# Pooled attention with a feed-forward layer: one weight conversion step on ACT instead of DVE, roundings of weights at another place of a step, other due times in the first and last pairs

## The chip, the cores and the metric

The kernel runs on one core of a Trainium2 chip. The metric is the time of the program on the device in microseconds (us). The engines are PE (matrix multiply), DVE (vector), ACT (scalar and activation functions), POOL (GpSimd) and SP, which here only issues transfers.

## The reference

```python
# attention: B, H, S, D = 4, 8, 1152, 64; q and k are scaled by about 0.71
q_pool = q.reshape(B, H, S // 2, 2, D).mean(axis=3)
scores = scale * np.matmul(q_pool, k.transpose(0, 1, 3, 2))
scores = scores - np.max(scores, axis=-1, keepdims=True)
attn = np.exp(scores)
attn = attn / (np.sum(attn, axis=-1, keepdims=True) + 1e-09)
attn_out = np.matmul(attn, v)
# feed-forward: x is attn_out as 2304 tokens x 512; w_in 512 x 2048, w_out 2048 x 512
h = np.maximum(x @ w_in, 0.0)
return h * h @ w_out
```

All data are 32 bits. The kernel computes each product in three matmuls of rounded halves: a value x is split into a rounded high half and the low half x - high.

## The kernel before

The work has two parts. The **attention** part goes over 16 pairs of heads, n = 0 to 15, and in each over two halves of the pooled queries, e = 0 and 1; (n,e) is called a half pair here. For a pair, `prep` (four steps u) transposes keys and queries on PE into PSUM banks; `prep_high` on ACT and `prep_low` on DVE write the two halves. For a half pair, `scores` gives nine chunks c on PE, each in a PSUM bank; `evict` brings a chunk to SBUF, six of the nine on DVE (L381, with a running maximum) and three on ACT (L378); `max_copied` (L385) takes the maximum of those three. `max_fin` (L327), a transposition on PE (`max_turn`) and `max_rows` (L343) make of it the shift of the exponentials. ACT takes the exponentials in place, in six instructions (`expo`, L389). POOL adds exponentials of several chunks (`add`, L432), so that the sum (`total`, L439) needs fewer matmuls; the half pairs (n,0) have four additions, (n,1) three, pair 15 none and two. `pv` (L404) multiplies with the values; `total_x` (ACT, then DVE L452 and L453) inverts the sum, and `pv_x` (L465) writes the result into `xt`. PSUM has four banks for `scores`, `prep`, the maxima and the open sums together.

The **feed-forward** part goes over steps (i, f): block i of the tokens (256, then four of 512) and slice f of 128 of the 2048 inner columns, in five passes of 2, 3, 4, 4 and 3 slices over all blocks. A step is `layer1` (12 matmuls, then on ACT g = relu, square, and the rounded half `gh`, and `gl` on DVE) and `layer2` of the step two before it (12 matmuls for a full block). At the end of a pass over a block the accumulators are copied out of PSUM, by ACT in the first pass (L693), by DVE in the others (L695); the next block needs their banks. `split_x` makes the halves of a block of x, ACT (L160) and DVE (L161).

The weights come as whole 32-bit units u = 0 to 31 (512 columns of 128 rows; even u are of `w_in`, odd of `w_out`) and are converted by `convert`, six steps: L122 the absolute value, L124 a maximum, L127 a shift, L130 and L134 bits, L136 a product into `r`, which POOL then adds to (L138). Its buffer `a` is single: L122 of a unit writes what L136 of the unit before reads. `split_w` rounds the converted weight on ACT (L148) and subtracts, on DVE for u < 4 and on POOL after that (L149). Units 0 to 3 are converted in the attention part: 0 and 1 during pairs 0 to 2, 2 and 3 during pair 15. The others are converted one pass ahead of their use.

The order of the attention part is written by a planner: `at` gives every operation a due time from the tables `AT` (L21) and `BT` (L28), never earlier than the operations that it must follow, and `plan` (L503) emits them sorted by due time. Each engine works its queue in that order. In the feed-forward part (L716 to L743) the operations are traced step by step; a scheduler may reorder them on an engine, while a conversion step is kept behind all that is traced before it on its engine (`keep_in_program_order`).

Of the kernel before, what the change touches and what calls it, by code (L numbers as in the profile page):

```python
# [8 lines left out]
F32 = mybir.dt.float32  # L9
# [4 lines left out]
ACTF = mybir.ActivationFunctionType  # L14
ALU = mybir.AluOpType
# [10 lines left out]
    u3=2.1607, vs=0.025, x0=0.0686, x1=0.3357, xg=0.2377,  # L26
)
BT = dict(  # L28
    u0=2.461, u1=-0.052, u2=1.778, u3=2.34, c0=2.06, c1=2.959, c2=-0.148, c3=1.446, cs=0.404, x=-1.613,
    w0=-2.307, w1=-1.838, s0=-0.109, s1=-0.104, v0=0.619, v1=2.469, t0=-5.963, t1=-1.1, lastn=3, lv=-3.166,  # L30
    pq=-0.498, s2=0.089, s3=0.001, v2=-0.001, lastm=9, t2=-0.385, p0=1.161, p1=0.934, wd=0.681, w=0.073,
    v3=-0.582, t3=-1.202, p2=0.017, p3=-0.048, y0=0.536, y1=0.082, y2=0.119, y3=0.466, d0=0, d1=-0.024,
)
WARM = 24
SOON = 3
# [5 lines left out]
def kernel(  # L41
# [9 lines left out]
    nc = tc.nc  # L51
# [26 lines left out]
    def run(ctx, exact):  # L78
# [18 lines left out]
        WB = 6  # L97
        NU = 2 * KF
        NCV = 6
# [4 lines left out]
        def load_raw(u):  # L104
            f, half = divmod(u, 2)
            t = cv.tile([P, CW, 2], I32, tag="raw", name="raw", bufs=2)
            if half == 0:
                nc.sync.dma_start(out=t.rearrange("p (k f) e -> p k f e", k=KD),
                                  in_=WI[:, 2 * f * P:2 * (f + 1) * P].rearrange("(k p) (f e) -> p k f e", p=P, e=2))
            else:  # L110
                nc.sync.dma_start(out=t, in_=WO[f * P:(f + 1) * P, :].rearrange("p (d e) -> p d e", e=2))
            raw[u] = t

        def convert(u, part):
            if part == 0:
                cvt[u] = [cv.tile([P, CW], I32, tag="a", name="a"), cv.tile([P, CW], I32, tag="h", name="h", bufs=2),
                          wfp.tile([P, CW], F32, tag="r", name="r")]
            a, h, r = cvt[u]
            lo, hi = raw[u][:, :, 0], raw[u][:, :, 1]
            if part == 0:  # L120

                i = nc.vector.tensor_scalar(out=a, in0=hi, scalar1=0x7FFFFFFF, scalar2=None, op0=ALU.bitwise_and)  # L122
            elif part == 1:
                i = nc.vector.tensor_scalar(out=a.bitcast(F32), in0=a.bitcast(F32), scalar1=TINY, scalar2=None, op0=ALU.max)  # L124
            elif part == 2:

                i = nc.vector.tensor_scalar(out=a, in0=a, scalar1=3, scalar2=0x3FFFFFF8, op0=ALU.logical_shift_left,  # L127
                                            op1=ALU.bitwise_and)
            elif part == 3:
                i = nc.vector.scalar_tensor_tensor(out=h, in0=hi, scalar=-0x40000000, in1=a, op0=ALU.bitwise_and,  # L130
                                                   op1=ALU.bitwise_or)
            elif part == 4:

                i = nc.vector.tensor_scalar(out=a, in0=h, scalar1=-0x800000, scalar2=None, op0=ALU.bitwise_and)  # L134
            else:
                i = nc.vector.scalar_tensor_tensor(out=r, in0=lo.bitcast(U32), scalar=2.0 ** -52, in1=a.bitcast(F32),  # L136
                                                   op0=ALU.mult, op1=ALU.mult)
                nc.gpsimd.tensor_tensor(out=r, in0=r, in1=h.bitcast(F32), op=ALU.add)  # L138
                wf[u] = r
                del cvt[u], raw[u]  # L140
            return i

        def split_w(u, pool, tag, bufs):

            f, half = divmod(u, 2)
            x = wf.pop(u)
            w = pool.tile([P, 2, CW], F32R, tag=tag, name=tag, bufs=bufs)
            nc.scalar.copy(out=w[:, 0], in_=x)  # L148
            (nc.vector if u < CU else nc.gpsimd).tensor_tensor(out=w[:, 1], in0=x, in1=w[:, 0], op=ALU.subtract)  # L149
            (wo if half else wi)[f] = w  # L150
# [18 lines left out]
        with ExitStack() as a:  # L169
# [5 lines left out]
            lv = a.enter_context(tc.tile_pool(name="lv", bufs=2))  # L175
# [461 lines left out]
        wp = ctx.enter_context(tc.tile_pool(name="wp", bufs=WB))  # L637
# [75 lines left out]
        work = {}  # L713
# [10 lines left out]
        for n in range(len(steps) + 2):  # L724
            for u, j in work.get(n, []):
                if j < NCV:
                    if j == 0 and u + 1 < NU:
                        load_raw(u + 1)
                    tc.keep_in_program_order(convert(u, j))
                else:  # L730
                    split_w(u, wp, "w" + "io"[u % 2], WB)
            if n < len(steps):
                i, f, p = steps[n]
                if f == P0[p] + 1 and n + PASS[p] - 1 < len(steps):
                    split_x(turns[turns.index((i, p)) + 1][0], xh_p)
                layer1(i, f)
            if n >= 2:
                layer2(*steps[n - 2][:2])
            if n == NB * PASS[0] and not exact:
                judge()  # L740

# [2 lines left out]
    with ExitStack() as c:  # L744
        run(c, False)
# [33 lines left out]
```

## Time and profile before

| | us |
|---|---|
| runs | 786.03, 786.09, 787.78 (median 786.09) |
| profiled execution | 785.6 |
| its span | 783.5 |
| PE busy | 740.1 (94%) |
| DVE busy | 589.4 (75%) |
| ACT busy | 498.2 (64%) |
| POOL busy | 400.4 (51%) |

The span runs from the first to the last instruction of the profiled execution; 2.1 us lie around it. The attention part lasts to about 375 us, the feed-forward part from there to the end. A timeline row gives the start, the duration, the operation, and in brackets how long the engine had been idle before it and what ended that.

### The profile page before, as it was taken

To read this page: it belongs to the slowest core of one execution; us is meant where nothing else is said; L and a number is where in the kernel's file an instruction comes from. 1 tells how busy PE (TensorE), PEld (TensorE's weight loads), DVE (VectorE), ACT (ScalarE), POOL (GpSimd) and SP (SyncE) were. 2 spreads that over 40 slices of the span, in tenths; PEclk is the share of its full clock that TensorE was granted. 3 is DMA by queue.
4 is the path that set the end of the run, shared out by engine and by line. 5 is a ranking of instruction groups with operands and counts; after the bars stand their busy time and mean duration, and the time that the engine had idled before them with its cause. 6 is when DMAs were issued, how large, how long until landed. Compare 5 with 4: busy or idle time off the path is not lost.

```text
span 783.5 us, 14050 instructions
## 1 busy us (share of the span) xinstructions
PE 740.1 (94%) x5514; PEld 579.8 (74%) x5514; DVE 589.4 (75%) x1095; ACT 498.2 (64%) x794; POOL 400.4 (51%) x176
## 2 busy tenths in 40 slices
PE   8768999999999999989989999999999999999996
PEld 7546666777776667666767788888888888888885
DVE  6988999999999999987997997676645655434432
ACT  3748888888888888974856654454444544444431
POOL 1758999999999999985253343122121311110000
PEclk9999999999999999999999999999999999999998
DMA  9233333333222333000121121011100100000312
GB/s 264 63 88 89 92 92 92 92 91 85 78 68 63 77 91 92 32 32 28 55 80 55 55 80 54 28 55 54 54 28 27 55 28 27 1 2 5 103 55 85
DMA packets 62091, 50.80 MB, mean 65 GB/s; under 512 B 39232, under 2 KB 49472, under 8 KB 62016
## 3 DMA queue, kind: packets, MB, share of 16 engines
q1 hardware_dynamic: 60656, 47.59, 22.1%
q10 hardware_dynamic: 1360, 2.23, 0.9%
q8 instruction: 45, 0.74, 0.4%
q14 instruction: 30, 0.25, 0.1%
HBM read 45.09 MB, written 4.72 MB: 64 GB/s over the span
## 4 chain that ended last, share of the span: by engine, by line
PE 68%; DVE 20%; ACT 4%; issue 4%; POOL 3%; DVEq 0%; POOLq 0%; ACTq 0%
PE o L687 22%; PE h L652 21%; PE s L404 11%; PE s L362 10%; DVE p L381 6%; DVE pm L385 4%; POOL ts L432 3%; ACT p L389 2%; PE s L439 1%; DVE xlo L161 1%; PE s L251 1%; DVE r L136 1%; DVE a L134 1%; DVE h L130 1%; PE s L624 1%
## 5 line engine op out<-in xcount | busy, mean ns | idle before, releaser
L389 ACT ACTIVATE p<-p,nb 128x864 f32<-128x864 f32 x192 | 184.4, 1009 | 31.1 <-DVE nb L343 31.0
L652 PE MATMUL h<-xhi,wi 128*128 128x512 f32 (+1 forms) x600 | 170.0, 368 | 0.0
L687 PE MATMUL o<-wo,gh 128*128 128x512 f32 x540 | 166.7, 390 | 1.2 <-DVE part L695 1.2
L138 POOL TENSOR_TENSOR r<-r,h 128x512 f32<-128x512 f32 x32 | 46.1, 1439 | 205.0 <-DVE r L136 193.3
L381 DVE TENSOR_SCALAR_CACHE_REDUCE p<-s 128x576 f32<-128x576 f32 x192 | 138.4, 755 | 11.5 <-PE s L362 7.0
L404 PE MATMUL s<-p,vt 128*64 128x288 f32 x1080 | 143.6, 409 | 0.0
L362 PE MATMUL s<-qq,kk 64*128 64x288 f32 x1728 | 132.1, 301 | 7.4 <-ACT p L378 3.1
L362 PEld LDWEIGHTS s<-qq,kk 64*128 64x128 f32 x1728 | 118.5, 186 | 23.4 <-issue 13.4
L432 POOL TENSOR_TENSOR ts<-p 128x1728 f32<-128x1728 f32 x31 | 120.3, 3880 | 25.4 <-ACT p L389 24.2
L652 PEld LDWEIGHTS h<-xhi,wi 128*128 128x128 f32 x600 | 109.6, 188 | 19.9
L432 POOL TENSOR_TENSOR ts<-ts,p 128x1728 f32<-128x1728 f32 x31 | 122.2, 3943 | 3.7 <-ACT p L389 1.3
L659 DVE TENSOR_TENSOR gl<-g,gh 128x512 fp32r<-128x512 f32 (+1 forms) x80 | 55.3, 692 | 89.3 <-ACT gh L658 89.0
L687 PEld LDWEIGHTS o<-wo,gh 128*128 128x128 f32 x540 | 100.5, 188 | 21.8 <-issue 1.6
L404 PEld LDWEIGHTS s<-p,vt 128*64 128x64 f32 x1080 | 78.4, 137 | 45.6 <-issue 0.5
L652 PE MATMUL h<-xlo,wi 128*128 128x512 f32 (+1 forms) x300 | 110.3, 368 | 0.0
L687 PE MATMUL o<-wo,gl 128*128 128x512 f32 x270 | 105.0, 389 | 0.0
L654 ACT ACTIVATE g<-h 128x512 f32<-128x512 f32 (+1 forms) x80 | 44.2, 553 | 64.9 <-PE h L652 61.0
L161 DVE TENSOR_TENSOR xlo<-xt,xhi 128x1024 fp32r<-128x1024 f32 (+7 forms) x40 | 58.8, 1486 | 32.6 <-ACT xhi L160 32.6
L658 ACT CAST gh<-g 128x512 fp32r<-128x512 f32 (+1 forms) x80 | 46.3, 579 | 51.2 <-PE o L687 45.2
L378 ACT COPY p<-s 128x576 f32<-128x576 f32 x96 | 59.5, 637 | 22.5 <-PE s L362 20.4
L432 POOL TENSOR_TENSOR ts<-ts 128x576 f32<-128x576 f32 x45 | 64.7, 1437 | 3.5
L652 PEld LDWEIGHTS h<-xlo,wi 128*128 128x128 f32 x300 | 56.5, 188 | 9.3
(84 smaller groups left out, 888.7 us busy)
## 6 DMA issues: line engine op xcount, KB each, us to landing
kt<-in_k_dram SPq DMA_DIRECT2D x32, 288.0 KB, 6.1
vt<-in_v_dram SPq DMA_DIRECT2D x16, 576.0 KB, 3.9
qt<-in_q_dram SPq DMA_DIRECT2D x16, 512.0 KB, 5.1
raw<-in_moe_w_in_dram SPq DMA_DIRECT2D x16, 512.0 KB, 3.8
raw<-in_moe_w_out_dram SPq DMA_DIRECT2D x16, 512.0 KB, 3.3
out_dram<-part SPq DMA_DIRECT2D x19, 128.0 KB, 2.9
out_dram<-part ACTq DMA_DIRECT2D x17, 128.0 KB, 3.4
ql<-in_q_dram SPq DMA_DIRECT2D x16, 64.0 KB, 5.0
```

The costliest lines, as they stand in the source:

```text
L138: nc.gpsimd.tensor_tensor(out=r, in0=r, in1=h.bitcast(F32), op=ALU.add)
L161: nc.vector.tensor_tensor(out=l, in0=x, in1=h, op=ALU.subtract)
L362: nc.tensor.matmul(out=s[:, h, :NH], lhsT=l[rows(h)], rhs=r[rows(h)], start=(i == 0), stop=(i == len(terms) - 1))
L378: nc.scalar.copy(out=y, in_=x)
L381: nc.vector.tensor_scalar(out=y, in0=x, scalar1=1.0, scalar2=None, op0=ALU.mult, op1=ALU.max, accum_out=PM[n % 2][:, e, i:i + 1])
L389: nc.scalar.activation(out=p, in_=p, func=ACTF.Exp, bias=NB_[n % 2][:, e:e + 1])
L404: i = nc.tensor.matmul(out=t[rows(h), 0, :NH], lhsT=ld_["v", n][:, h, c, :], rhs=chunk(n, e, c)[:, h], start=(c == 0), stop=(c == NC - 1))
L432: nc.gpsimd.tensor_tensor(out=t[:, o], in0=t[:, o] if x is None else p_[n, e, x], in1=t[:, y] if isinstance(y, slice) else p_[n, e, y], op ...
L652: nc.tensor.matmul(out=h, lhsT=w, rhs=x, start=(m == 0), stop=(m == len(mm) - 1))
L658: nc.scalar.copy(out=gh, in_=g)
L659: nc.vector.tensor_tensor(out=gl, in0=g, in1=gh, op=ALU.subtract)
L687: nc.tensor.matmul(out=acc[i][t], lhsT=g, rhs=w, start=(first and m == 0), stop=(last and m == 2))
```

## The change

Three things change. L122 of every unit becomes an activation (Abs) on ACT. The call of `split_w` for the units of the feed-forward part stands behind the step's `layer1` and `layer2` instead of ahead of them. And some thirty due times in `BT` are others; the line in the loop that uses `wd` and `w` moves the conversions of the first pass later by 0.55 of a step, and their `split_w` by 0.2.

```diff
--- before.py
+++ after.py
@@ -26,10 +26,10 @@
     u3=2.1607, vs=0.025, x0=0.0686, x1=0.3357, xg=0.2377,
 )
 BT = dict(
-    u0=2.461, u1=-0.052, u2=1.778, u3=2.34, c0=2.06, c1=2.959, c2=-0.148, c3=1.446, cs=0.404, x=-1.613,
-    w0=-2.307, w1=-1.838, s0=-0.109, s1=-0.104, v0=0.619, v1=2.469, t0=-5.963, t1=-1.1, lastn=3, lv=-3.166,
-    pq=-0.498, s2=0.089, s3=0.001, v2=-0.001, lastm=9, t2=-0.385, p0=1.161, p1=0.934, wd=0.681, w=0.073,
-    v3=-0.582, t3=-1.202, p2=0.017, p3=-0.048, y0=0.536, y1=0.082, y2=0.119, y3=0.466, d0=0, d1=-0.024,
+    u0=2.381, u1=-0.694, u2=1.981, u3=0.786, c0=2.065, c1=2.14, c2=-0.077, c3=1.327, cs=0.404, x=-0.767,
+    w0=-2.786, w1=-1.83, s0=-0.12, s1=-0.111, v0=0.414, v1=0.694, t0=-5.822, t1=-1.297, lastn=3, lv=-2.351,
+    pq=0.782, s2=0.067, s3=0.002, v2=-0.001, lastm=9, t2=-0.12, p0=2.149, p1=0.092, wd=0.337, w=0.619,
+    v3=-0.858, t3=-0.511, p2=0.001, p3=-0.366, y0=1.692, y1=0.259, y2=0.022, y3=0.452, d0=-0.077, d1=-0.057,
 )
 WARM = 24
 SOON = 3
@@ -119,7 +119,7 @@
             lo, hi = raw[u][:, :, 0], raw[u][:, :, 1]
             if part == 0:
 
-                i = nc.vector.tensor_scalar(out=a, in0=hi, scalar1=0x7FFFFFFF, scalar2=None, op0=ALU.bitwise_and)
+                i = nc.scalar.activation(out=a.bitcast(F32), in_=hi.bitcast(F32), func=ACTF.Abs)
             elif part == 1:
                 i = nc.vector.tensor_scalar(out=a.bitcast(F32), in0=a.bitcast(F32), scalar1=TINY, scalar2=None, op0=ALU.max)
             elif part == 2:
@@ -727,8 +727,6 @@
                     if j == 0 and u + 1 < NU:
                         load_raw(u + 1)
                     tc.keep_in_program_order(convert(u, j))
-                else:
-                    split_w(u, wp, "w" + "io"[u % 2], WB)
             if n < len(steps):
                 i, f, p = steps[n]
                 if f == P0[p] + 1 and n + PASS[p] - 1 < len(steps):
@@ -736,6 +734,9 @@
                 layer1(i, f)
             if n >= 2:
                 layer2(*steps[n - 2][:2])
+            for u, j in work.get(n, []):
+                if j == NCV:
+                    split_w(u, wp, "w" + "io"[u % 2], WB)
             if n == NB * PASS[0] and not exact:
                 judge()
```

Sorted by their due times, these operations change their place in a queue (all else keeps its order, and SP's queue is the same):

- DVE: `evict` (0,1) of chunks 2 and 6 ahead of `prep_low` (1,2); `prep_low` (1,0) ahead of `max_fin` (0,1); L130 of unit 0 ahead of the third eviction of (1,0) instead of behind it. L124, L127, L130 and L134 of unit 1, then the sum's steps and `pv_x` of (0,1), stand in a row ahead of the evictions of (1,1), and L136 of unit 1 behind the first of these instead of ahead of the evictions of (2,0). The subtraction of `split_w` 0 goes ahead of the last eviction of (14,0), and `split_x` of block 0 from behind `max_copied` (14,1) to ahead of `max_copied` (15,0).
- ACT: L122 of units 0 to 3 among the exponentials of (0,0), (1,0), (15,0) and behind those of (15,1); `prep_high` (1,2), (1,3) and (2,2) each past one or two exponentials; `total_x` (0,1) ahead of the second group of exponentials of (1,0); the roundings of `split_w` 0 and `split_x` as on DVE.
- PE: the last three `pv` and the `total` of (0,1) ahead of the scores of (1,1).
- POOL: L138 of unit 1 ahead of the additions of pair 1; L138 of unit 2 behind those of (15,1).

## Rows read from the trace of the kernel before

**Rows 1.** Windows: span, busy us (instructions) of each engine, clock, DMA share, GB/s.

```profile
27.00:64.50 37.50, 25.02 (x265) 16.80 (x266) 33.50 (x65) 21.97 (x34) 26.46 (x10) 1.00 0.24 62
...
64.50:315.00 250.50, 242.12 (x2660) 176.89 (x2660) 230.98 (x525) 218.92 (x346) 236.64 (x85) 0.99 0.35 86
...
315.00:365.00 50.00, 44.74 (x465) 31.71 (x465) 44.05 (x91) 40.98 (x61) 38.35 (x15) 1.00 0.11 35
...
400.00:445.00 45.00, 41.72 (x196) 33.23 (x195) 38.15 (x49) 29.09 (x54) 18.76 (x11) 1.00 0.21 67
...
500.00:600.00 100.00, 100.00 (x471) 83.92 (x470) 62.01 (x96) 48.31 (x80) 22.19 (x17) 1.00 0.13 43
```

**Rows 2.** Timeline of PE, start: start us, us, operation, [idle before, releaser].

```profile
42.85 0.27 PE L251 MATMUL s<-ident,pb 64*128 64x64 f32 x2 [3.35 <-DVE pb L327]
...
59.41 0.27 PE L251 MATMUL s<-ident,pb 64*128 64x64 f32 x2 [2.88 <-DVE pb L327]
```

**Rows 3.** Timeline of DVE, start: conversion steps of units 0 and 1.

```profile
26.53 0.66 DVE L124 TENSOR_SCALAR a<-a 128x512 f32<-128x512 f32 x1
...
30.78 0.45 DVE L127 TENSOR_SCALAR a<-a 128x512 int32<-128x512 int32 x1
...
38.98 3.66 DVE L134 TENSOR_SCALAR a<-h 128x512 int32<-128x512 int32 x1
...
58.78 0.42 DVE L134 TENSOR_SCALAR a<-h 128x512 int32<-128x512 int32 x1
...
62.75 1.02 DVE L136 SCALAR_TENSOR_TENSOR r<-raw,a 128x512 f32<-128x512 uint32 x1
```

**Rows 4.** Timeline of POOL, start: the additions of half pairs (0,0) and (0,1).

```profile
23.02 3.89 POOL L432 TENSOR_TENSOR ts<-p 128x1728 f32<-128x1728 f32 x1 [8.53 <-ACT p L389]
...
26.98 3.96 POOL L432 TENSOR_TENSOR ts<-ts,p 128x1728 f32<-128x1728 f32 x1
...
31.02 2.99 POOL L432 TENSOR_TENSOR ts<-ts 128x576 f32<-128x576 f32 x2
...
34.58 3.86 POOL L432 TENSOR_TENSOR ts<-p 128x1728 f32<-128x1728 f32 x1 [0.57 <-DVE h L130]
...
38.52 3.83 POOL L432 TENSOR_TENSOR ts<-ts,p 128x1728 f32<-128x1728 f32 x1
```

**Rows 5.** Timeline of ACT, start: one exponential of (0,1).

```profile
33.49 1.02 ACT L389 ACTIVATE p<-p,nb 128x864 f32<-128x864 f32 x1
```

**Rows 6.** Groups by line: out<-in, shape xcount, then busy us, mean ns, idle before.

```profile
L122 DVE TENSOR_SCALAR a<-raw 128x512 int32<-128x512 int32 x32 | 16.3, 510 | 0.4
...
L148 ACT CAST wo<-r 128x512 fp32r<-128x512 f32 x15 | 9.3, 621 | 29.9 <-POOL r L138 29.9
...
L404 PE MATMUL s<-p,vt 128*64 128x288 f32 x1080 | 143.6, 409 | 0.0
...
L617 ACT ACT_TABLE_LOAD x1 | 1.3, 1283 | 0.7 <-PEq L764 0.7
```

**Rows 7.** Timelines of DVE, PE and POOL: pairs 14 and 15.

```profile
334.30 1.21 DVE L161 TENSOR_TENSOR xlo<-xt,xhi 128x1024 fp32r<-128x1024 f32 x1
...
336.32 0.27 PE L251 MATMUL s<-ident,pb 64*128 64x64 f32 x2 [1.41 <-DVE pb L327]
...
343.87 3.87 POOL L432 TENSOR_TENSOR ts<-p 128x1728 f32<-128x1728 f32 x1 [1.61 <-ACT p L389]
```

**Rows 8.** Timelines of ACT and PE: feed-forward part.

```profile
401.54 0.62 ACT L148 CAST wi<-r 128x512 fp32r<-128x512 f32 x1 [3.48 <-POOL r L138]
...
422.18 0.62 ACT L148 CAST wo<-r 128x512 fp32r<-128x512 f32 x1 [5.03 <-POOL r L138]
...
403.19 0.73 PE L687 MATMUL o<-wf,gh 128*128 128x512 f32 x2 [2.21 <-ACT part L693]
...
425.50 0.72 PE L687 MATMUL o<-wf,gh 128*128 128x512 f32 x2 [0.90 <-ACT part L693]
...
448.53 0.70 PE L687 MATMUL o<-wo,gh 128*128 128x512 f32 x2 [1.16 <-DVE part L695]
```

## The prediction

> **What bounds the kernel now.** I read the windows first [rows 1]: they split the span by stage, and TensorE (PE) is the engine to follow. From 500 to 600 us it is busy for all of 100 us; nothing that DVE, ACT or POOL does there can move the end. From 64.5 to 315 us it is busy for 242.12 of 250.50, in a cycle that repeats pair after pair. Idle time is left at the start (12.5 us between 27 and 64.5), in the last two pairs (5.3 us between 315 and 365) and in the first pass of the feed-forward part (3.3 us between 400 and 445). PE's own work is the same before and after, so the change is worth the idle time of PE that it takes away or adds in these three places.
>
> The next view is PE's timeline, which names what ended each wait. At the start the two large ones end with `max_fin`, the small reduction that gives a half pair its shift: 3.35 and 2.88 us [rows 2]. DVE's timeline tells why [rows 3]: the L134 step of weight unit 0, 0.42 us where it runs freely, lasts 3.66 us from 38.98, and `max_fin` of half pair (1,0) stands behind it. POOL's timeline has the reason [rows 4]: its addition from 38.52 lasts 3.83 us, to 42.35, and L134 ends 0.29 us after it. L124 and L127 end 0.28 and 0.29 us after POOL's additions that end at 26.91 and 30.94. So a conversion step on DVE that comes while a POOL addition runs waits for the end of that one addition, and gets in ahead of the next. What such a step costs hangs on which side of a boundary between two additions it arrives. L134 came 0.54 us after the boundary at 38.44.
>
> **The start, pairs 0 to 2.** I followed each queue in its new order with the durations of the rows.
> 1. L122 of unit 0 leaves DVE, and two evictions move ahead of `prep_low` (1,2), which waits for ACT. DVE reaches L124 about half a us earlier than 26.53. POOL's first addition still runs to 26.91, since the exponentials that release it keep their place; L124 ends at 27.19 as before. This gain is lost there.
> 2. `prep_low` (1,0), 0.60 us, now stands ahead of `max_fin` (0,1). The shift of (0,1) comes 0.6 us later; `prep` (1,1), behind the transposed maximum on PE, and ACT's copy of it move by as much, and so does L127 behind them: from 30.78 to about 31.37. There the next addition has begun (31.02, the first of two that take 2.99 us, so it ends near 32.47). L127, which waited 0.16 us, waits 1.1, and the evictions of (1,0) start 1.5 us later.
> 3. L130 of unit 0, one eviction earlier than before, no longer waits 0.8 us there. L134 then arrives near 39.7, against 38.98.
> 4. ACT's exponential that releases the addition of 34.58 ended at 34.51 [rows 5]. It is behind the shift (0.6 us) and an eviction that waits for a PSUM bank: 0.7 to 1.1 us later. The boundary that L134 needs moves from 38.44 to between 39.1 and 39.55. So L134 misses it again, by 0.2 to 0.6 us, and waits for an addition that ends 0.7 to 1.1 us later than before: `max_fin` (1,0) at +0.75.
> 5. In half pair (1,1) three PV steps of (0,1) and the sum move ahead of the scores: 3 x 4 matmuls of 0.133 (143.6 us for 1080) and 8 of about the same, 2.6 us [rows 6]. For this, the sum's DVE steps, L130 and L134 of unit 1 are done before the evictions instead of between them and `max_fin` (1,1). The two nearly cancel; L122 of unit 1 on ACT (0.62 against 0.43, and two hops) leaves about +0.45.
> 6. L136 of unit 1, 1.02 us at 62.75 behind a POOL addition [rows 3], stood ahead of the evictions of pair 2. It is done long before: -0.95.
> Sum: 0.75 + 0.45 - 0.95, about **+0.3 us**. Bounds: +1.2 (point 6 hidden) and -3.4, if L134 makes its boundary: `max_fin` (1,0) then comes 3.6 us earlier in place of 0.75 later, less what the POOL addition then costs L136 of unit 0 (at most 1.4 us), with point 6 on top. From pair 2 the orders are the same up to pair 13, and the cycle carries the shift on.
>
> **The price of L122 on ACT.** The trace has no Abs. Nearest rows [rows 6]: the cast of the same 128x512 from SBUF on ACT, 0.62 us, the strided read on DVE, 0.51 on average. Bounds 0.5 to 1.24 (a stride that halves the rate); I take 0.62. In the attention part it comes four times, ahead of exponentials that have at least 0.3 us to spare, except in half pair (15,1), counted below. Against this move speaks the Trainium skill, "ScalarE: Activation LUTs", section "Rules for kernel authors", which gives cheap arithmetic to VectorE; rows agree when DVE is free (0.43 against 0.62). By that rule alone the 28 later units would cost 28 x 0.2 = 5.3 us; they lie beside a PE that is busy throughout, so the sum would not change.
>
> **Pairs 14 and 15.** `split_x` of block 0 leaves pair 14. There its DVE half took 1.21 us at 334.30, ahead of `max_fin` (14,1), and PE waited 1.41 us where 0.27 is usual [rows 7]: -1.1. It returns ahead of `max_fin` (15,0), which has no slack: +1.1. It comes there some 0.9 us before the addition at 343.87, which its own ACT half (1.05 us) also delays, so I count no wait on POOL. `split_w` of unit 0 goes 5 us earlier, onto DVE ahead of the last eviction of (14,0), behind a short addition: some 0.9 us later there, of which 0.6 us is slack on PE, and less work later. L122 of unit 2 leaves DVE (hidden there) and costs ACT 0.52 us ahead of the evictions of (15,1). Sum **+0.5 us**; bounds -1.1 (all of it hidden) and +3.9 (`split_x` meets the 3.87 us addition).
>
> **The feed-forward part.** PE's waits are 2.21, 0.90 and 1.16 us [rows 8]. The first: ACT sits idle 3.48 us before the rounding of a converted weight (L148, 401.54), until POOL has finished that weight; in the queue behind it stand g and the copies of the accumulators, whose last matmuls PE had finished before the wait, and PE waits for these copies (L693 ends its wait). The second is alike (L148 at 422.18, idle 5.03). At the end of the step the rounding is traced behind both, so these waits can go, 3.1 us at most. The third ends with an addition on DVE behind conversion steps; L122 off DVE takes about 0.5 of it. Against this: six more ACT instructions of 0.62 in that pass, each after L136 of the unit before, since the buffer `a` is single, and conversion starts that move by half a step. I take **-2.0 us**; bounds -3.6 (both waits and the 0.5) and +1.0.
>
> **Sum**: 0.3 + 0.5 - 2.0 = -1.2 on the profiled 785.6 (span 783.5): 784.4. Two of the three runs shown stand 0.45 above the profiled one (median 786.09), so 784.8 on their scale.
>
> **Rivals.**
> - *L134 makes its boundary* (0.2 to 0.6 us are missing, and the start is worth -3.4 instead of +0.3): 781.1. For it: a margin this small hangs on which bank an eviction gets, and no row names banks. Against: point 2 rests on four rows in a line. Chance 0.26.
> - *The roundings give nothing*, because ACT's order doesn't follow the place in the code, or the copies wait behind g: 786.8. For it: in this part ACT's order is not that of the code (a split of x stands long before its step). Chance 0.18.
> - *The new Abs stalls ACT* (slower): it is pinned behind what is traced on ACT and ahead of g; if ACT reaches it before DVE has finished L136 of the unit before, g and the copies wait as they do now behind L148. Five units of that pass have such a predecessor; 5 x 2.21 = 11 us, no gain of 2.0: 797; 789 with one stall in three. It decides once the stall is longer than the 2.5 us that PE works on a layer (12 matmuls of 0.212, 100.00 us for 471 in [rows 1]) without needing ACT; L136 in the rows ends soon after the DVE work of the step before, so it mostly won't. Chance 0.08.
> - *Abs needs a table of its own*: the profile has one table load of 1.28 us [rows 6]; one for each of the four units of the attention part and one back to the exponentials would be 8 x 1.28 = 10 us on ACT, most of it ahead of exponentials. Chance 0.02, 795. The same page, section "Table sets", says that abs is in every set; no run here shows it yet.
>
> **How the numbers follow.** The forecast, 0.46, has 782.5 to 787 as its own range. The range 780.0 to 788.0 takes in the first two rivals (the first down to 1.1 below its time) and leaves out the two slow ones and the tails, about 0.2. A measurement can tell about 0.3% from no change: below 783.7 is faster, above 788.4 slower. Faster: 0.28 of the forecast, 0.95 of the first rival: 0.39. Slower: the last two and little of the others: 0.12. The rest, 0.49, is no change.
>
> **What would show it.** Point 2: L127 near 31.4, longer than 1 us. Point 4: L134 again over 3 us; if it lasts 0.5, the first rival. Point 6: no L136 at the start of pair 2. Pair 14: the 1.41 us wait of PE gone, one of about 1 at `max_fin` (15,0). Feed-forward: no PE wait that ends with a copy L693. The prediction is wrong above all if a conversion step falls on the other side of a POOL boundary than I count.

## The result and the profile after

The changed kernel took 779.67 us in the median (777.05 to 782.07, 7 runs), the kernel before 786.66 (784.99 to 787.78, 7 runs): a ratio of 0.9911, 95% interval 0.9891 to 0.993. A second set gave 777.56 against 786.09, ratio 0.9895 (0.9873 to 0.9918). (A ratio and its interval are those on record; they need not be the quotient of the two medians.) The forecast was 784.8, the range 780.0 to 788.0: the kernel gained about 7 us or more where 1.2 was forecast.

The windows of the changed kernel, in the stretches of [rows 1]: span, busy us (instructions) of PE, its weight loads, DVE, ACT and POOL, then the granted clock, DMA share, GB/s.

```profile
27.00:64.50 37.50, 29.27 (x268) 20.66 (x270) 29.69 (x66) 22.85 (x35) 26.84 (x11) 0.82 0.28 79
64.50:315.00 250.50, 241.82 (x2672) 176.48 (x2672) 231.14 (x527) 219.33 (x346) 236.74 (x84) 1.00 0.33 84
315.00:365.00 50.00, 45.22 (x460) 31.53 (x458) 40.98 (x87) 41.49 (x62) 37.38 (x15) 1.00 0.11 36
400.00:445.00 45.00, 44.49 (x211) 36.66 (x212) 36.16 (x50) 35.00 (x62) 18.82 (x12) 1.00 0.21 71
```

The idle time of PE went from 12.5 to 8.2 us at the start and from 3.3 to 0.5 in the feed-forward window. But at the start the granted clock is 0.82 where it was 1.00: part of the freed time was filled by a slower PE. A window table can't tell where the end moved, so I compared the same instruction in both traces. `max_fin` of half pair (5,0) shows what the start is worth (the cycle of the pairs then carries the shift on), the first `g` (L654) what is left after pair 15, and the `g` of step 40 what the feed-forward part adds.

```profile
376.31 0.38 ACT L654 ACTIVATE g<-h 128x256 f32<-128x256 f32 x1
...
569.07 0.59 ACT L654 ACTIVATE g<-h 128x512 f32<-128x512 f32 x1
```

In the kernel before these two stand at 377.22 and 575.08. The profiled 5.6 us of span (783.5 to 777.9) divide so:

| | forecast | this trace | second trace of the same kernel |
|---|---|---|---|
| start, to (5,0) | +0.3 | -1.0 | -3.0 |
| pairs 14 and 15 | +0.5 | +0.1 | 0.0 |
| feed-forward, to step 40 | -2.0 | -5.1 | -5.1 |
| later | 0 | +0.4 | +0.4 |

All of this is measured against one trace of the kernel before. Two kernels of the experiments below (the first two) have its attention part unchanged, and their traces reach (5,0) 1.3 and 1.8 us later than it, with the granted clock at 0.50 for 6.8 and 13.7 us of the start instead of 3.4. So a figure for the start holds to about 2 us; the feed-forward figure is the same in both traces of the changed kernel.

The start of the changed kernel, on DVE (L127 to L327), POOL (L432), ACT (L389) and PE (L251), answering to [rows 2 to 5]:

```profile
31.25 1.36 DVE L127 TENSOR_SCALAR a<-a 128x512 int32<-128x512 int32 x1
...
33.89 0.68 DVE L130 SCALAR_TENSOR_TENSOR h<-raw,a 128x512 int32<-128x512 int32 x1
...
39.66 0.41 DVE L134 TENSOR_SCALAR a<-h 128x512 int32<-128x512 int32 x1
39.99 0.15 DVE L327 TENSOR_REDUCE pb<-pm 128x1 f32<-128x7 f32 x1
...
35.68 3.86 POOL L432 TENSOR_TENSOR ts<-p 128x1728 f32<-128x1728 f32 x1 [1.79 <-ACT p L389]
40.74 3.85 POOL L432 TENSOR_TENSOR ts<-ts,p 128x1728 f32<-128x1728 f32 x1 [1.20 <-issue]
...
38.70 1.91 ACT L389 ACTIVATE p<-p,nb 128x864 f32<-128x864 f32 x2
...
42.83 0.27 PE L251 MATMUL s<-ident,pb 64*128 64x64 f32 x2
```

L134, 3.66 us long before, takes 0.41, and `max_fin` of (1,0) comes at 39.99 instead of 42.56. The boundary between POOL's additions is at 39.54 (35.68 + 3.86), L134 comes 0.12 us after it, and yet is free: the next addition starts only at 40.74, since its exponentials end at 40.61. All the same PE takes the turn of that maximum at 42.83, as it did before (42.85): it is still at the matmuls ahead of it, at half its clock. The second trace of the same kernel has that turn 1.6 us earlier. Windows of PE alone (span, busy us, granted clock, DMA share, GB/s), first the trace above:

```profile
34.00:38.00 4.00, 3.83 (x34) 0.53 0.10 32
38.00:41.00 3.00, 3.00 (x24) 0.50 0.00 0
```

and the second one, with its turn:

```profile
34.00:38.00 4.00, 4.00 (x40) 0.57 0.12 42
38.00:41.00 3.00, 3.00 (x32) 1.00 0.00 0
...
41.21 0.27 PE L251 MATMUL s<-ident,pb 64*128 64x64 f32 x2
```

In the first, PE runs at 1.2 GHz (granted clock 0.50) from 34.3 to 41.1, in the second from 34.0 to 37.4.

In the feed-forward part one wait of PE is left of the three of [rows 8], and on ACT the roundings (L148) stand behind the copies:

```profile
398.74 0.68 ACT L122 ACTIVATE a<-raw 128x512 f32<-128x512 f32 x1 [1.34 <-DVE r L136]
...
402.73 0.67 ACT L148 CAST wi<-r 128x512 fp32r<-128x512 f32 x1
...
407.57 0.62 ACT L148 CAST wo<-r 128x512 fp32r<-128x512 f32 x1 [0.71 <-POOL r L138]
...
422.54 0.62 ACT L148 CAST wo<-r 128x512 fp32r<-128x512 f32 x1 [0.26 <-POOL r L138]
...
400.43 0.73 PE L687 MATMUL o<-wf,gh 128*128 128x512 f32 x2 [0.86 <-ACT part L693]
```

### The profile page after: what moved, and what is told of

Its sections match the earlier page's. It is cut to its first block, busy times and chain, and to the rows that moved or that the text cites. A ratio compares the mean times of both kernels' runs of the same rounds, so it can differ in the third digit from the quotient of the medians.

```text
span 777.9 us, 14031 instructions
## 1 busy us (share of the span) xinstructions
PE 742.3 (95%) x5514; PEld 582.8 (75%) x5514; DVE 569.2 (73%) x1063; ACT 515.9 (66%) x826; POOL 400.0 (51%) x176
## 3 DMA queue, kind: packets, MB, share of 16 engines
q10 hardware_dynamic: 1360, 2.23, 0.9%
## 4 chain that ended last, share of the span: by engine, by line
PE 74%; DVE 17%; ACT 3%; issue 2%; POOL 2%; DVEq 0%; POOLq 0%; ACTq 0%
PE o L687 23%; PE h L652 23%; PE s L404 12%; PE s L362 11%; DVE p L381 7%; DVE pm L385 5%; POOL ts L432 2%; PE s L251 1%; PE s L439 1%; ACT p L389 1%; PE s L624 1%; PE c L404 1%; DVE a L124 1%; DVE qq L293 1%; DVE h L130 1%
## 5 line engine op out<-in xcount | busy, mean ns | idle before, releaser
L389 ACT ACTIVATE p<-p,nb 128x864 f32<-128x864 f32 x192 | 184.3, 1008 | 27.4 <-DVE nb L343 27.4
L138 POOL TENSOR_TENSOR r<-r,h 128x512 f32<-128x512 f32 x32 | 51.7, 1617 | 174.7 <-DVE r L136 170.4
L362 PE MATMUL s<-qq,kk 64*128 64x288 f32 x1728 | 134.2, 304 | 6.1 <-ACT p L378 2.9
L432 POOL TENSOR_TENSOR ts<-p 128x1728 f32<-128x1728 f32 x31 | 120.4, 3884 | 32.2 <-ACT p L389 32.2
L362 PEld LDWEIGHTS s<-qq,kk 64*128 64x128 f32 x1728 | 120.3, 188 | 22.2 <-issue 13.4
L432 POOL TENSOR_TENSOR ts<-ts,p 128x1728 f32<-128x1728 f32 x31 | 121.1, 3905 | 3.6 <-issue 1.2
L659 DVE TENSOR_TENSOR gl<-g,gh 128x512 fp32r<-128x512 f32 (+1 forms) x80 | 58.6, 733 | 83.3 <-ACT gh L658 83.0
L654 ACT ACTIVATE g<-h 128x512 f32<-128x512 f32 (+1 forms) x80 | 44.2, 552 | 62.1 <-PE h L652 59.2
L161 DVE TENSOR_TENSOR xlo<-xt,xhi 128x1024 fp32r<-128x1024 f32 (+7 forms) x40 | 56.1, 1412 | 37.9 <-ACT xhi L160 37.9
L432 POOL TENSOR_TENSOR ts<-ts 128x576 f32<-128x576 f32 x45 | 64.3, 1429 | 3.5
L695 DVE TENSOR_TENSOR part<-part,o 128x512 f32<-128x512 f32 x72 | 48.4, 686 | 21.5 <-PE o L687 21.5
```

What stands on the lines that cost most here:

```text
L161: nc.vector.tensor_tensor(out=l, in0=x, in1=h, op=ALU.subtract)
L362: nc.tensor.matmul(out=s[:, h, :NH], lhsT=l[rows(h)], rhs=r[rows(h)], start=(i == 0), stop=(i == len(terms) - 1))
L389: nc.scalar.activation(out=p, in_=p, func=ACTF.Exp, bias=NB_[n % 2][:, e:e + 1])
L432: nc.gpsimd.tensor_tensor(out=t[:, o], in0=t[:, o] if x is None else p_[n, e, x], in1=t[:, y] if isinstance(y, slice) else p_[n, e, y], op ...
L659: nc.vector.tensor_tensor(out=gl, in0=g, in1=gh, op=ALU.subtract)
L695: nc.vector.tensor_tensor(out=y, in0=y, in1=acc[i][t], op=ALU.add)
```

## The experiments

### The feed-forward part, one edit at a time

The roundings at the end of the step, alone, on the kernel before:

```diff
-                else:
-                    split_w(u, wp, "w" + "io"[u % 2], WB)
...
                 layer2(*steps[n - 2][:2])
+            for u, j in work.get(n, []):
+                if j == NCV:
+                    split_w(u, wp, "w" + "io"[u % 2], WB)
```

> The kernel before with one part of the change alone: the roundings of the feed-forward units traced at the end of the step. Theory W (roundings): PE's waits of 2.21 and 0.90 us that end with the copies L693 go, and with each the slow pace of the three banks behind it (1.0 instead of 0.68 us per bank, about 0.8 us a time): the feed-forward part becomes 3.5 to 5 us shorter, the kernel about 782.5. Rival D (due times): this alone gives nothing, the moved conversion starts do it: 786.5. What was forecast: 2.0 us.

Measured: 787.69 against 786.09, ratio 1.0007 (0.9993 to 1.0022); the feed-forward part became 1.2 us longer, all of it in a stretch of low clock (below). ACT (L148) and PE of this kernel:

```profile
410.81 0.62 ACT L148 CAST wo<-r 128x512 fp32r<-128x512 f32 x1 [6.12 <-POOL r L138]
...
423.46 0.62 ACT L148 CAST wo<-r 128x512 fp32r<-128x512 f32 x1 [5.03 <-POOL r L138]
...
413.92 0.73 PE L687 MATMUL o<-wf,gh 128*128 128x512 f32 x2 [0.72 <-ACT part L693]
426.79 0.74 PE L687 MATMUL o<-wf,gh 128*128 128x512 f32 x2 [2.32 <-ACT part L693]
```

A window of PE alone there (span, busy us, granted clock, DMA share, GB/s):

```profile
428.30:431.70 3.40, 3.40 (x10) 0.50 0.00 0
```

The first stall is gone (that rounding now stands behind the copies), but the next rounding, of a `wo`, waits 6.12 us ahead of `gh`, a split of x and the next copies, where it waited 2.72 before; and the one at 423.46 has kept its place and its 5.03. So the roundings' place does not by itself give the 2.0 us that I had put on it, nor the 3.5 to 5 of theory W: what it gains at the first stall is lost again at the two behind it, and at 1.2 GHz PE then loses another 1.3 us against the same matmuls of the kernel before.

The due times of the first pass alone (`wd=0.337, w=0.619` in the kernel before):

> The kernel before with wd and w of the change alone (conversions of the first pass 0.55 of a step later, their roundings 0.2 later, still traced ahead of the layers). Theory W: the roundings still stand ahead of g, so waits of the same kind remain, perhaps at other steps: 785 to 788. Rival D: the feed-forward part becomes about 5 us shorter, the kernel about 781.5.

Measured: 787.45, ratio 1.0005 (0.9982 to 1.0027); feed-forward 1.0 us longer, with the waits 2.23, 1.92 and 1.16 us. As theory W has it; rival D falls.

L122 on ACT alone:

> The kernel before with L122 on ACT alone, everything else in its old place. Theory W: nothing in the feed-forward part beyond 0.5 us at the third wait (1.16 us behind DVE), and at the start only what one instruction of 0.4 us on DVE is worth there: 785.5 to 787. Rival A (the gain comes from DVE's relief): the feed-forward part becomes 3 us or more shorter: 783.5 or less. Each L122 lasts 0.66 us or so on ACT, and no table load is added.

Measured: 790.26, ratio 1.0048 (1.0031 to 1.0065): neither theory. The trace is that of its longest run (794.75). In it (5,0) is 2.5 us later than in the kernel before, and the feed-forward part became 4.4 us longer; one wait of PE before the copies is 4.05 us, and from its end on the clock is low for 6.8 us (a window of PE, as above):

```profile
407.70:414.50 6.80, 6.04 (x14) 0.50 0.24 75
```

L122 lasts 0.67 us and the profile has the same single table load.

Then parts of the changed kernel undone. Its feed-forward edits undone (roundings ahead of the layers, old `wd` and `w`; L122 on ACT):

> The changed kernel with the feed-forward part's own two edits undone (roundings ahead of the layers, old wd and w); L122 stays on ACT, the attention part is the changed one. L122 on ACT alone cost 4.4 us in the feed-forward part. Theory W (place and due times together give the gain): feed-forward 4 to 5 us longer than before, start as in the changed kernel: 787 to 789. Rival (what L122 on ACT cost came from the old order of pair 15): feed-forward within 1 us of before: 783 to 785.

Measured: 787.9, ratio 1.0034 (1.0018 to 1.005), in theory W's range; feed-forward 3.3 us longer than before where theory W had 4 to 5, with a wait of 4.02 us. Only the roundings put back ahead of the layers:

> The changed kernel with the roundings back ahead of the layers; L122 on ACT, wd and w stay as changed. Theory W (place and due times together): at least one rounding stands ahead of g and of the copies again, with PE waits of 1 to 2.5 us that end with L693: feed-forward 3 to 6 us longer than in the changed kernel, 781 to 784. Rival D (with L122 on ACT the due times do it alone): as the changed kernel, 777 to 780.

Measured: 787.38, ratio 1.0024 (1.0006 to 1.0041); feed-forward 5.0 us longer than before, 10.1 longer than in the changed kernel, where theory W had 3 to 6 and 781 to 784. Rival D falls. ACT and PE there:

```profile
400.98 0.62 ACT L148 CAST wi<-r 128x512 fp32r<-128x512 f32 x1 [4.59 <-POOL r L138]
401.50 0.66 ACT L122 ACTIVATE a<-raw 128x512 f32<-128x512 f32 x1
...
403.20 1.22 PE L687 MATMUL o<-wf,gh 128*128 128x512 f32 x2 [4.79 <-ACT part L693]
```

The rounding that waits for POOL now holds L122 too, and behind both stands `g` and all four copies. Only L122 back on DVE:

> The changed kernel with L122 back on DVE; place of the roundings, wd, w and all other due times as changed. Theory W: the feed-forward gain of 5 us stays but for about 1 us (the third wait, behind DVE): 778 to 781. Rival A (the gain needs DVE relieved of L122 and of its waits behind POOL): most of the gain is lost, 782 to 786.

Measured: 783.92, ratio 0.9981 (0.9961 to 1.0001); feed-forward 3.1 us shorter than before, so L122 on ACT is worth 2.0 of the 5.1. By its time this is rival A's range (782 to 786); the rest of the loss lies ahead of the feed-forward part, in pair 15 (below). The second rounding is the one that waits:

```profile
410.74 0.62 ACT L148 CAST wo<-r 128x512 fp32r<-128x512 f32 x1 [6.26 <-POOL r L138]
...
413.85 0.73 PE L687 MATMUL o<-wf,gh 128*128 128x512 f32 x2 [1.20 <-ACT part L693]
```

In the changed kernel that rounding waits 0.71 (407.57). Only `wd` and `w` old:

> The changed kernel with the old wd and w: roundings at the end of the step and L122 on ACT stay. In the runs so far each rounding that ACT waits for ahead of a step's copies has another cure: the first (idle 3.5 us, then 2.21 on PE) goes with the place, the second (6 us once the place is changed) with L122 on ACT, the third (5.0 us) with place and later due times together. Theory I (three cures): here the third stall alone returns, a rounding with 3 to 5 us of idle time before it and a wait of PE of 0.9 to 2.3 us that ends with L693: feed-forward 1.5 to 3.5 us longer than in the changed kernel, 779 to 782. Rival (place and L122 on ACT are enough): feed-forward as in the changed kernel.

Measured: 780.42, ratio 0.9936 (0.9912 to 0.996); feed-forward 3.0 us shorter than before, 2.1 less than in the changed kernel. The size is that of theory I, the mechanism is not: the third rounding waits 2.76 us but holds nobody up; what PE waits for is L122.

```profile
409.88 0.67 ACT L122 ACTIVATE a<-raw 128x512 f32<-128x512 f32 x1 [2.15 <-DVE r L136]
...
411.56 0.74 PE L687 MATMUL o<-wf,gh 128*128 128x512 f32 x2 [1.22 <-ACT part L693]
```

ACT came to L122 before DVE had finished L136 of the unit before, and `g` and the copies stood behind: the stall of my slow rival, once. All shifts of the feed-forward part together (first `g` to step 40, against the kernel before; each from one trace):

| roundings at the end | new `wd`, `w` | L122 on ACT | us |
|---|---|---|---|
| yes | | | +1.2 |
| | yes | | +1.0 |
| | | yes | +4.4 (old attention part), +3.3 (new) |
| | yes | yes | +5.0 |
| yes | yes | | -3.1 |
| yes | | yes | -3.0 |
| yes | yes | yes | -5.1 |

The three gains, the +1.0 and the kernel before are at full clock throughout. The other four are not: PE is at 1.2 GHz for 3.4 us in the +1.2 and the +3.3, for 6.8 us in the +4.4 and the +5.0, and loses 1.1 to 2.1 us there against the same matmuls of the kernel before. So the size of these losses is in part the clock's, and only their sign is used here.

Each edit alone loses or gives nothing, any two that hold the first give 3, all three 5.

### The due times of the attention part

All of `BT` but `wd` and `w`, with L122 on DVE and the old feed-forward part:

> The kernel before with the due times of the attention part alone (all of BT but wd and w); L122 on DVE, the feed-forward part in its old order. Theory S (the start comes from the due times): first g 1 to 3 us earlier than before, depending on the clock, with pairs 14 and 15 at about 0; feed-forward 0; in all 784 to 785.5. Rival A (L122 on ACT frees DVE there): with L122 back on DVE, L134 of unit 0 arrives 0.4 us later, in a POOL addition, and waits 3 us: nothing gained at the start, 786 or more.

Measured: 787.4, ratio 1.0027 (1.0009 to 1.0045): slower, which neither theory had, though the start is 2.7 us ahead at (5,0) and L134 nearly free (0.55 us), so rival A falls there. Pair 15 gives 3.0 back, part of it with the clock at 1.2 GHz (349.6 to 353.0). DVE and PE there, then ACT and POOL of the changed kernel at the same place:

```profile
345.85 3.48 DVE L122 TENSOR_SCALAR a<-raw 128x512 int32<-128x512 int32 x1
...
350.05 3.58 PE L362 MATMUL s<-qq,kk 64*128 64x288 f32 x30 [2.83 <-DVE p L381]
```

```profile
348.15 0.66 ACT L122 ACTIVATE a<-raw 128x512 f32<-128x512 f32 x1
...
346.96 3.93 POOL L432 TENSOR_TENSOR ts<-ts,p 128x1728 f32<-128x1728 f32 x1
```

In its new place L122 of unit 2 stands on DVE ahead of the evictions of (15,1) and waits for a POOL addition; on ACT it runs in the middle of one and takes its 0.66 us. The Trainium skill, "SBUF — State Buffer", section "Who interferes with whom", has both: DVE and POOL share a pair of ports that one of them locks for a whole instruction, if the DVE instruction is in a 2-port mode (as `tensor_scalar`, which L122 is, can be) or has two inputs in SBUF; and "PE and ACT never wait on anyone". The traces agree, with 3.48 against 0.66, though none names the mode that L122 runs in.

### The start

L134 of unit 0 moved in the kernel before, behind the maximum and the shift of (1,0):

```diff
-... + (BT[f"d{u}"] if u < 2 and j > 2 else 0), ("cv", u, j), convert, ...
+... + (BT[f"d{u}"] if u < 2 and j > 2 else 0) + (.12 if (u, j) == (0, 4) else 0), ("cv", u, j), convert, ...
```

> The kernel before with one instruction moved: L134 of unit 0 behind the maximum and shift of half pair (1,0) on DVE instead of ahead of them, so that its wait for POOL no longer stands before them. Theory L (this wait is the start's price): max_fin of (1,0) comes near 39.1 instead of 42.56, PE's wait of 3.35 us goes, and from pair 5 on the run is 2 to 3 us ahead of a run of before at the same clock: 783 to 784.5. Rival C (the clock takes it back): PE then has less idle time but its clock falls there, and pair 5 is within 1 us of before: 785.5 to 787. Rival N (the next wait takes its place): the evictions of (1,1) or L136 of unit 0 get the wait: within 1 us as well, at full clock.

Measured: 782.47 against 785.53, ratio 0.9976 (0.9959 to 0.9992), 3.6 us ahead at (5,0). L134 still waits (40.05, 2.79 us), but behind `max_fin` (39.08) it stops nobody. That one wait was the start's price: theory L (its trace is one of the faster; by the ratio the edit is worth about 1.9 us).

Now why L134 is free in the changed kernel. First `prep_low` of (1,0) put back behind `max_fin` and the shift of (0,1) (`u0=2.461` in the changed kernel), which brings L127 back in time:

> The changed kernel with one pair of DVE instructions in its old order: prep_low of (1,0) behind max_fin and the shift of (0,1). Theory P (the late L127 is what lets L134 through): L127 comes at 30.8, just ahead of POOL's boundary, the evictions of (1,0) are 1 to 1.5 us earlier, the exponential and the POOL addition that follows it too (34.6 instead of 35.7 to 36.3), while L134 still comes at 39 or later: it misses the boundary, lasts 3 us or more, and max_fin of (1,0) is back near 42.5: pair 5 about 2.5 us later than in the changed kernel, 780 to 782. Rival (L134 moves with the boundary): it stays free, and the run is as the changed kernel or 0.5 us faster.

Measured: 776.14, ratio 0.9888 (0.9867 to 0.9909), 5.3 us ahead at (5,0). Theory P fell: POOL's additions are earlier, and L134 with them. By the ratios this kernel isn't told apart from the changed one (0.9895).

```profile
30.39 0.47 DVE L127 TENSOR_SCALAR a<-a 128x512 int32<-128x512 int32 x1
32.14 0.68 DVE L130 SCALAR_TENSOR_TENSOR h<-raw,a 128x512 int32<-128x512 int32 x1
37.91 0.47 DVE L134 TENSOR_SCALAR a<-h 128x512 int32<-128x512 int32 x1
38.30 0.15 DVE L327 TENSOR_REDUCE pb<-pm 128x1 f32<-128x7 f32 x1
...
34.22 3.88 POOL L432 TENSOR_TENSOR ts<-p 128x1728 f32<-128x1728 f32 x1
38.18 3.93 POOL L432 TENSOR_TENSOR ts<-ts,p 128x1728 f32<-128x1728 f32 x1
```

Here L134 comes 0.19 us before the boundary at 38.10. What is common to this and the changed kernel is L130, one eviction earlier and free (0.68 us, against 1.32 at 33.24 in the kernel before). That alone, in the kernel before:

```diff
+... - (.03 if (u, j) == (0, 3) else 0), ("cv", u, j), convert, ...
```

> The kernel before with L130 of unit 0 alone moved, ahead of the third eviction of (1,0) instead of behind it (as in the changed kernel). Theory M (this moves L134 across POOL's boundary): L130 comes near 32.5, between POOL's two short additions, and takes 0.7 instead of 1.32 us; L134 comes about 0.6 us earlier, at 38.3 to 38.4, ahead of the boundary at 38.44, lasts 0.5 us, and max_fin of (1,0) stands near 38.9 instead of 42.56; pair 5 is 2 to 4 us earlier than in runs of before, 782.5 to 784. Rival S (the boundary is bound to the late exponentials, not to L130): L130 meets the second short addition, waits 1 us or more, the evictions behind it move, and L134 misses its boundary again: 785 to 788.

Measured: 781.94 against 786.12, ratio 0.994 (0.9925 to 0.9956), 2.9 us ahead at (5,0). Theory M. In this trace L127 missed its boundary too, so L130 came later than expected, but free, and the boundary moved too, from 38.44 to 39.70. L134 came 0.11 us ahead of it and ended 0.30 after it:

```profile
31.42 1.11 DVE L127 TENSOR_SCALAR a<-a 128x512 int32<-128x512 int32 x1
33.81 0.68 DVE L130 SCALAR_TENSOR_TENSOR h<-raw,a 128x512 int32<-128x512 int32 x1
39.59 0.41 DVE L134 TENSOR_SCALAR a<-h 128x512 int32<-128x512 int32 x1
...
35.83 3.87 POOL L432 TENSOR_TENSOR ts<-p 128x1728 f32<-128x1728 f32 x1 [2.01 <-ACT p L389]
```

### The clock

The changed kernel again:

> The changed kernel once more, for a second trace and more times. Theory C (the granted clock took the place of the wait): in the trace that we have, L134 of unit 0 is free (0.41 us at 39.66), but PE runs at 1.2 GHz from 34.4 to 41.0 and reaches the turn of the maximum of (1,0) at 42.83, as before (42.85). Where the clock stays at 2.4 GHz in that stretch, L134 is free too and the turn comes near 40.2, so the run takes about 777; where it falls, about 780. Rival B (POOL's boundary): L134 is free only because the slow clock made POOL's second addition wait for its exponential (the gap from 39.54 to 40.74); at full clock the gap closes, L134 lasts over 3 us, and those runs are the slow ones (near 782), not the fast ones.

Measured: 777.56 (776.89 to 782.21). L134 is free here as well (39.70, 0.41 us) and the low stretch is 3.4 us long instead of 6.8, the turn of (1,0) at 41.21, (5,0) at -3.0 instead of -1.0: as theory C has it in direction.

Rival B is neither shown nor excluded. Six traces have this start (three of them with feed-forward edits undone, one with the transposes below): L134 comes between 0.21 us ahead of the boundary and 0.12 us behind it, and in all six PE is at 1.2 GHz somewhere between 32 and 41, where the copy (L286) waits for it that stands ahead of the next addition's exponentials. None has the clock high throughout. And of the 13 runs of the changed kernel two, 782.07 and 782.21, took some 5 us more than those at 777, at mean granted clocks (0.993 and 0.992) as high as theirs (0.989 to 0.993). The mean clock doesn't tell them apart; a missed boundary, 3 to 4 us, would fit. No trace of such a run was kept.

Idle transposes on PE where it waits for `max_fin` (1,1):

```diff
-FILL = 8, 12, 24
+FILL = 8, 12, 24, 0, 22
...
-                        if n < 1:
+                        if n < 1 or (n, e) == (1, 1):
```

> The changed kernel with 22 more idle transposes on PE ahead of the turn of half pair (1,1), where PE waits 3.4 us for max_fin and its clock then falls to 1.2 GHz for 4 to 7 us. Theory C (the fall follows the idle stretch, and it costs time): the second stretch of low clock goes or moves, and pair 5 comes 1 to 2 us earlier than in runs of the changed kernel: 776 to 777.5. Rival F (the fall costs nothing, since PE waits for DVE at the start of pair 2 anyway): as the changed kernel, 777 to 780. Rival B (the transposes need a bank that comes free late): PE comes to the turn later, 0.5 to 2 us lost.

Measured: 777.11 (776.34 to 777.71), ratio 0.9892 (0.9871 to 0.9912). The low clock between 57 and 65 is gone, the time isn't told apart from the 777.56 of the changed kernel. Both start edits together:

> The two start edits that were faster than the changed kernel, together: prep_low of (1,0) behind max_fin and the shift of (0,1), and 22 idle transposes ahead of the turn of (1,1). Theory C (the low clock after PE's idle stretch costs time): no low clock between 50 and 65, 0.5 to 1.5 us faster than with the first edit alone (776.1): 774.7 to 775.6. Rival F (it costs nothing here): 775.5 to 776.5.

Measured: 775.9 (774.77 to 776.12), ratio 0.9863 (0.9845 to 0.9881), the fastest of all, beside 776.14 (0.9888) without the transposes: not told apart. This trace has no low clock anywhere at the start:

```profile
27.00:65.00 38.00, 30.87 (x340) 22.58 (x342) 33.59 (x74) 26.79 (x41) 31.21 (x13) 1.00 0.40 106
```

So the second stretch of low clock costs nothing that can be measured here (rival F): from `max_fin` (1,0) to (5,0) the kernel with it (`u0` alone, 55.4 to 58.8) takes 90.32 us, the one without 90.28. PE has waits of its own at the start of pair 2 that can take it up.

## Why the prediction was wrong, point by point

The first trace's span is 4.4 us shorter than the forecast had it: 3.1 us of that is the feed-forward term, 1.3 the start, 0.4 pairs 14 and 15, less 0.4 later. In the second trace the start misses by 3.3 and the feed-forward term by 3.1 again. So two terms failed: the feed-forward one in its size and in its reason, and point 4 of the start.

**What bounds.** The three places were right, and so was the worth of the steady pairs: the shift is -0.99 at (5,0) and -0.96 at (13,1).

**Start, points 1 to 3: right.** L124 ends at 27.10 (27.19 forecast), L127 comes at 31.25 and waits about a us (31.37 and 1.1), L130 is free, L134 comes at 39.66 (39.7). What point 2 costs was seen with `u0`: without it, (5,0) is 2.3 us earlier than in the second trace; by the ratios of the runs that isn't told apart.

**Point 4: the step of the start that failed.** The boundary is at 39.54, inside the 39.1 to 39.55 forecast, so L134 is 0.12 us late, not 0.2 to 0.6. And I let the next addition follow at the boundary, as in [rows 4]. Its exponentials stand behind a copy (L286) that waits for PE, here until 38.20 where it was 35.80 in the kernel before, and the addition starts 1.2 us after the boundary. In the other traces with the new due times L134 comes 0.1 to 0.3 us ahead of the boundary, or up to 0.12 after it with POOL not ready. L134 was moved by L130, as I had counted (point 3), and I still put the chance of the rival at 0.26 with a margin of 0.2 us. In the traces of the changed kernel L134 does miss the boundary, as I had said, and is free because POOL isn't ready; with PE at half its clock ahead of that copy this is in part luck. The price, 3.4, was about right: 3 us by the second trace, 1 in the first, which has twice the low clock.

**Point 5: right within half a us; point 6: the size came out, the cause isn't shown.** From the turn of (1,0) to `max_fin` (1,1) the changed kernel loses 0.1 (0.45 forecast). L136 of unit 1 is now at 53.23, and from `max_fin` (1,1) to (2,1) this trace gains 1.1 us and the second 1.6 (0.95 forecast). But the two kernels with L134 or L130 of unit 0 alone moved gain 0.9 there too, with L136 in its old place: once the start is earlier it takes 0.73 us instead of 1.02 (60.43, with L134 moved). So by these traces its move is worth 0.1 to 0.6 us, and the agreement with 0.95 is luck.

**L122 on ACT.** Two rows by group, changed kernel: busy us, mean ns, idle before.

```profile
L122 ACT ACTIVATE a<-raw 128x512 f32<-128x512 f32 x32 | 21.4, 670 | 17.6 <-DVE r L136 17.6
...
L617 ACT ACT_TABLE_LOAD x1 | 1.3, 1283 | 0.7 <-PEq L765 0.7
```

0.67 us for the 0.62 taken, and no further table load. The Trainium skill, "ScalarE: Activation LUTs", section "Table sets", says that abs is in every set; the single load agrees. But I had its worth as half a us. It is worth 2.0 in the feed-forward part, since the second conversion is ready about 3 us earlier, and it keeps about 3 us from being lost in pair 15. I read it as hidden there, which holds for the old place only.

**Pairs 14 and 15: right.** PE's two turns:

```profile
334.40 0.27 PE L251 MATMUL s<-ident,pb 64*128 64x64 f32 x2 [0.27 <-DVE pb L327]
...
345.36 0.27 PE L251 MATMUL s<-ident,pb 64*128 64x64 f32 x2 [0.90 <-DVE pb L327]
```

The wait of 1.41 is gone from pair 14, one of 0.90 (1.1 forecast) has come to pair 15; in all +0.1 instead of +0.5.

**Feed-forward: the term that failed most, mis-sized and for a wrong reason.** The forecast was -2.0, the bound -3.6, the measurement -5.1. Two things failed. First, the bound was the sum of PE's idle times. A bank that ACT releases late is followed by three more at ACT's pace, which the idle column doesn't show; PE of the kernel before, after its wait at 403.19:

```profile
404.20 0.74 PE L687 MATMUL o<-wf,gh 128*128 128x512 f32 x2
...
405.20 0.73 PE L687 MATMUL o<-wf,gh 128*128 128x512 f32 x2
...
406.00 0.62 PE L687 MATMUL o<-wf,gh 128*128 128x512 f32 x2
```

From 403.19 to 406.00 are 2.81 us for three banks, which elsewhere take 0.68 each: 0.77 more than the wait. By matching PE's instructions, the gain is 0.5 near 390 (where there was no idle time at all), 1.4 at the first wait (0.86 is left of 2.21, and its slow banks), 1.8 at the second (1.07 and its banks 0.75) and 1.4 at the third: 5.1. Second, I put the gain on the place of the roundings. Alone it gives nothing; the place, the due times and L122 on ACT each take away another stall, and undone in the changed kernel they cost 10.1 (part of it the clock's), 2.1 and 2.0 us.

**Rivals.** *L134 makes its boundary* is what happened in effect (L134 was free), though not by making the boundary in the two traces of the changed kernel; with the feed-forward part mis-sized its 781.1 was still too slow. *The roundings give nothing* holds for the roundings alone. *L122 stalls ACT*, whose 789 leaves out the lost 2.0 (with it 790.5), holds with the old `wd` and `w`, where L122 waits 2.15 us for L136 and PE 1.22. With the roundings ahead of the layers PE waits 4.0 to 4.8 us, but there ACT waits in L148, for POOL, and L122 only stands behind it. In the changed kernel L122 waits 1.34 us for L136 ahead of `g` (398.74) and PE 0.86. What the kernels with L122 on ACT do give back is 0.4 to 0.9 us near step 44; the one with it on DVE gives back nothing there. *A table of its own* fell.

What stays open: whether L134 is free in the changed kernel when PE's clock is high ahead of the boundary (rival B), and which PE or ACT instruction sets the length of the first stretch of low clock. Two traces of one kernel differ in it by 3.4 us, and in the start by 2.0; that the one makes the other is read from where PE stood, not from a run with that stretch alone changed.

## What to carry to other kernels

When an engine's instruction waits behind a lock that another engine holds for several us, look for the instruction before it in the queue that could come a few tenths earlier: one L130, moved past one eviction, was worth 4 us in the medians. Look at the margin in several traces, since it was a tenth of a us here. An edit that moves one of several stalls is not worth its share of the sum: the next stall in the queue takes over until all have their cure, so measure edits in combination too. And size a wait for a buffer by the time to the last of the buffers that follow it, not by the idle time before the first.

## What the runs showed of the hardware that I had not expected

In all traces but one of the sixteen PE's granted clock falls to 0.50 within the first 70 us, for 3.4 to 10.2 us in one stretch, and not at the same place in each execution. In the changed kernel it fell at 34.3 in one trace, 1.9 us after the end of a wait of 1.84 us, and at 34.0 in the other; and it fell again at 58.1 and 57.9, within a wait of 3.40 us. The same kernel's start differed by 2.0 us between these traces. With 22 idle transposes in that second wait the fall there did not come, in both traces that have them.
